# Choosing anew which groups VectorE makes, where they lie and which leave a step to GpSimd, with new pacing and scheduler constants, in a fused attention and FFN block

## The chip, the cores and the metric

One core of a Trainium2 chip runs the whole program. The metric is the device time of one execution in microseconds. Before the change the kernel took 773.14 us (median of three runs). PE is the matrix engine, ACT is ScalarE, DVE is VectorE, POOL is GpSimd. All runs told of here are of the state "fast".

## The reference, cut to what matters

```python
xn  = layernorm(x)                                   # 2048 x 512
qkv = xn @ wqkv                                      # 32 heads of 16
p   = softmax(q @ k.T / 4)                           # 32 heads x 2048 x 2048
A   = (p @ v) @ wo
h   = relu(xn @ W_gate) * (xn @ W_up)                # 2048 x 1792
out = x + A + h @ W_down
```

The exponential over 32 x 2048 x 2048 scores is the large job. ACT does most of it; the kernel gives a part to DVE.

## The kernel before: the parts that the change and the argument touch

A *group* is four heads x 512 queries x 128 keys: four tiles of 128 x 512. A *block* is one set of four heads and 512 queries, with 16 groups; there are 32 blocks and 512 groups. `D_POS` lists for each block the positions whose exponential DVE makes; all other groups go to ACT, as *units* of alternately three and two tiles. PV is the product of probabilities and V that consumes either kind; PE issues it in steps of four matmuls side by side. Units are counted from 0 in ACT's order.

```python
SLIP = 100.0                 # a tolerance in the scheduler, for GpSimd pieces beside DVE work
FILL = 0.72                  # below this share of PE work in a window, blank matmuls are put in
NRING = 6                    # places for finished exponentials: 6 of three tiles, 6 of two
P_PRIO = -2.4                # rank of GpSimd's pieces in the scheduler
POOL_AT = ((), (2,), (), (6,), ...)    # positions whose shifted pattern GpSimd makes
D_POS   = ((), (2, 3, 8, 11), (2, 8, 11, 15), ...)
PV_LAST = 10                 # over the last 10 units PV is preferred
O_BEG, F_PRE, F_BEG = 10, (1, 1, 1), 20     # pacing of output projection and FFN
```

DVE makes an exponential from bit patterns, in four evictions from PSUM and four passes over 128 x 2048:

```python
def dve_exp(g, u):
    for j, t in enumerate(t4):
        # PE: scores into one bank of ps_b            (L1202)
        # DVE: tensor_scalar, scores -> uint16 pattern (L1218), 4 per group
    # DVE: two pattern operations (L1229, L1231) and one product (L1233)
    if g in on_pool:
        # GpSimd: five tensor_tensor adds of about 205 int32 columns (L1237)
    else:
        # DVE: tensor_scalar add of SHIFT              (L1244)
    ...
```

ACT's exponentials write into the ring, and PV frees a place in it:

```python
tr = Tile("r%d" % u, P_ring[k0])                       # needs a free place
exp_ops[u] = G.op("ACT", 75 + 427 * n, ex, reads=[ts], writes=[tr], ...)      # L1279
G.op("PE", 225, pv, ..., prio=u + PV_LAG - (200 if u > NU - PV_LAST else 0))  # L1178
```

A list scheduler in the program turns all operations into one fixed order for each engine when the program is built; at run time each engine goes through its own order and waits on semaphores. So a constant such as `SLIP` does nothing on the chip but change that order.

The softmax here doesn't subtract the row's maximum and nothing guards it: scores larger than these inputs give would overflow.

## Time and profile before

| | before |
|---|---|
| median | 773.14 us (772.91 to 774.35) |
| profiled run | 771.55 us, span 769.8 us |
| ACT, exponentials alone | 737.6 us busy, 6.6 us idle ahead of them |
| DVE busy | 725.0 us |
| last exponential ends | 759.46 us |

The busy lines, the costliest groups, the stretches and ACT's waits are shown in the prediction. The end of the timeline gives the *tail*: after the last exponential come the last PV, two copies (L1105), sums, reciprocals, the spreading of them, the last projection, four adds, and the store. The lines are from the timelines of ACT and DVE in the kernel before; columns are start, length, instruction, and in brackets the idle time just before it and what ended it:

```profile
754.34 5.12 ACT L1279 ACTIVATE ring<-ps_sc 128x1536 bf16<-128x1536 f32 x5 [0.25 <-PE ps_sc L1202]
...
757.29 1.28 DVE L1244 TENSOR_SCALAR dring<-dring 128x2048 uint16<-128x2048 uint16 x2
...
761.11 0.75 DVE L1105 COPY Wv<-ps_b 128x256 f32<-128x256 f32 x2 [2.54 <-PE ps_b L1178]
```

### The profile page before, as it was taken

What the parts mean: (1) busy time and instruction counts of PE and PEld (TensorE: products, weight loads), DVE (VectorE), ACT (ScalarE), POOL (GpSimd) and SP (SyncE); (2) the same over time, 40 slices, a digit from 0 to 9 for tenths busy, and PEclk for the clock granted to TensorE, in tenths of its full rate; (3) what the DMA queues carried; (4) which work ended last, traced back from release to release, by engine and by line L of the source; (5) the groups of instructions that cost most, each with busy time, mean ns of one, the idle gap of its engine ahead of it and who ended that gap; (6) DMA issues with size and microseconds to landing.
All of it is one profiled execution on the core that took longest, in us unless ns stands there. A gap on an engine that the chain in (4) does not pass through costs nothing.

```text
span 769.8 us, 21666 instructions
## 1 busy us (share of the span) xinstructions
PE 748.2 (97%) x9482; PEld 228.2 (30%) x9482; DVE 725.0 (94%) x1132; ACT 746.0 (97%) x662; POOL 200.3 (26%) x253
## 2 busy tenths in 40 slices
PE   8999999999999999999999999999999999999997
PEld 3322322222222222222232222222222233222333
DVE  8699999999999899999988999998999979999696
ACT  6999999999999999999999999999999999999994
POOL 3112232422122232412323113232222223232120
PEclk9999999999999999999999999999999999999999
DMA  6312121202111122222220122232121113221100
GB/s 212 118 43 57 55 59 50 78 23 77 38 45 38 52 76 59 71 69 69 67 56 30 57 64 57 59 76 59 51 68 47 60 50 88 54 74 47 37 15 28
DMA packets 95757, 46.83 MB, mean 61 GB/s; under 512 B 69936, under 2 KB 91824, under 8 KB 95664
## 3 DMA queue, kind: packets, MB, share of 16 engines
q1 hardware_dynamic: 95664, 45.46, 21.5%
q8 instruction: 74, 1.21, 0.6%
q14 instruction: 19, 0.16, 0.1%
HBM read 36.70 MB, written 8.50 MB: 59 GB/s over the span
## 4 chain that ended last, share of the span: by engine, by line
DVE 48%; PE 42%; ACT 8%; issue 1%; DMA 0%; POOL 0%; DVEq 0%
DVE dring L1218 19%; PE ps_b L734 16%; PE ps_b L1178 12%; PE ps_sc L1202 11%; DVE dring L1233 8%; ACT ring L1279 7%; DVE dring L1229 5%; DVE dring L1231 4%; DVE dring L1244 3%; DVE up_sb L942 3%; PE ps_b L1202 2%; DVE hT L946 2%; DVE Wv L1112 2%; DVE qT L786 1%; DVE v_aug L828 1%
## 5 line engine op out<-in xcount | busy, mean ns | idle before, releaser
L1279 ACT ACTIVATE ring<-ps_sc 128x1536 bf16<-128x1536 f32 (+1 forms) x647 | 737.6, 1271 | 6.6 <-PE ps_b L1178 3.7
L1218 DVE TENSOR_SCALAR dring<-ps_b 128x512 uint16<-128x512 f32 x432 | 288.0, 683 | 16.7 <-PE ps_b L1202 15.4
L1202 PE MATMUL ps_sc<-qm,kT 32*128 32x512 bf16 x1616 | 260.5, 384 | 4.6 <-ACT ring L1279 2.8
L1202 PE MATMUL ps_b<-qm,kT 32*128 32x512 bf16 x432 | 161.9, 384 | 2.8 <-DVE dring L1218 1.8
L1178 PE MATMUL ps_b<-ring,v_aug 128*17 128x512 bf16 x1616 | 145.4, 381 | 5.7 <-DVE Wv L1112 4.6
L1233 DVE TENSOR_TENSOR dring<-dring 128x2048 bf16<-128x2048 bf16 x108 | 130.9, 1213 | 0.0
L1202 PEld LDWEIGHTS ps_sc<-qm,kT 32*128 32x128 bf16 x1616 | 62.0, 91 | 226.8 <-ACT ring L1279 196.9
L1130 POOL TENSOR_TENSOR rrec<-rsum,minus 128x16 f32<-128x16 f32 x30 | 93.2, 3106 | 110.3 <-DMA rsum<-Wv 110.3
L1140 POOL TENSOR_TENSOR x_sb<-Wv,rb 128x128 bf16<-128x128 f32 x100 | 45.8, 458 | 247.7 <-DVE dring L1233 87.8
L1178 PE MATMUL ps_b<-dring,v_aug 128*17 128x512 bf16 x864 | 79.5, 381 | 0.2 <-DVE dring L1231 0.2
L1178 PE MATMUL ps_b<-dring,vd 128*17 128x512 bf16 x864 | 78.6, 382 | 0.3 <-DVE dring L1233 0.2
L1229 DVE TENSOR_SCALAR dring<-dring 128x2048 uint16<-128x2048 uint16 x108 | 73.6, 683 | 0.5
L1231 DVE TENSOR_SCALAR dring<-dring 128x2048 uint16<-128x2048 uint16 x108 | 73.7, 685 | 0.0
L1237 POOL TENSOR_TENSOR dring<-dring,shift 128x205 int32<-128x205 int32 (+1 forms) x80 | 42.1, 527 | 108.9 <-DVE dring L1218 37.2
L734 PE MATMUL ps_b<-xnT,wus 128*32 128x512 bf16 x896 | 69.4, 384 | 0.5 <-DVE dring L1218 0.3
L734 PE MATMUL ps_b<-xnT,wgs 128*32 128x512 bf16 x896 | 69.3, 384 | 0.4
L1244 DVE TENSOR_SCALAR dring<-dring 128x2048 uint16<-128x2048 uint16 x92 | 62.0, 682 | 0.0
L1178 PEld LDWEIGHTS ps_b<-ring,v_aug 128*17 128x17 bf16 x1616 | 37.2, 89 | 64.7 <-issue 35.8
L1202 PEld LDWEIGHTS ps_b<-qm,kT 32*128 32x128 bf16 x432 | 38.5, 91 | 45.9 <-DVE dring L1218 29.8
L734 PE MATMUL ps_b<-Wd,hT 128*32 128x512 bf16 x672 | 49.4, 382 | 0.2
L942 DVE COPY up_sb<-ps_b 128x512 f32<-128x512 f32 x56 | 38.2, 681 | 0.0
L1178 PEld LDWEIGHTS ps_b<-dring,vd 128*17 128x17 bf16 x864 | 20.4, 89 | 33.9 <-issue 12.3
(111 smaller groups left out, 402.0 us busy)
## 6 DMA issues: line engine op xcount, KB each, us to landing
rb<-rec_scr SPq DMA_DIRECT2D x30, 256.0 KB
wus<-in_B_W_up_dram SPq DMA_DIRECT2D x56, 128.0 KB, 2.4
wgs<-in_B_W_gate_dram SPq DMA_DIRECT2D x56, 128.0 KB, 2.3
qm<-q_scr SPq DMA_DIRECT2D x30, 128.0 KB
o_scr<-x_sb SPq DMA_DIRECT2D x25, 128.0 KB
q_scr<-qT SPq DMA_DIRECT2D x17, 128.0 KB
xr_sb<-in_A_x_dram SPq DMA_DIRECT2D x16, 128.0 KB, 2.6
out_dram<-xn_sb SPq DMA_DIRECT2D x16, 128.0 KB, 1.9
```

Of the source, the lines that this page charges most:

```text
L734: ins = e.matmul(bank_of(tile, sub)[32 * j:32 * j + 32, :], st[:, 32 * j:32 * j + 32], mv, start=(i == 0), stop=(i == n - 1), tile_positio ...
L942: G.op("DVE", 610, lambda e: e.tensor_copy(up_sb[:, tup.slot, :], bank_of(tu)), reads=[tu], writes=[tup], prio=slots[1] + EV)
L1130: G.op("POOL", 3000, lambda e: e.tensor_tensor(rrec[:, par, :], rsum[:, par, :], minus[:, 0:1].to_broadcast([128, 16]), ALU.pow), reads=[t ...
L1140: o = G.op("POOL", 200 + 1080 // N_MUL, lambda e, a=w * k, b=w * k + w: e.tensor_tensor(oT_of(tn)[:, a:b], o_sb[:, to.slot, a:b], rb[:, tr ...
L1178: ins = e.matmul(ps_b[32 * j:32 * j + VN, 0, :], v, src[j][1](k), start=(first and k == 0), stop=(last and k == ways - 1), tile_position=( ...
L1202: return e.matmul(bank, kT[32 * j:32 * j + 32, gg, 128 * kt:128 * kt + 128], qm[32 * j:32 * j + 32, t_q[(c4, gg)].slot, ee, :], start=True ...
L1218: o = G.op("DVE", 610, lambda e, j=j, ts=ts: e.tensor_scalar(dring[:, tp.slot, 512 * j:512 * j + 512].bitcast(U16), ps_b[:, ts.slot, :], 0 ...
L1229: G.op("DVE", 600, lambda e: e.tensor_scalar(b(tm, U16), b(tp, U16), 0xFF80, None, op0=ALU.bitwise_or), reads=[tp], writes=[tm], prio=u - ...
L1231: G.op("DVE", 600, lambda e: e.tensor_scalar(b(tn, U16), b(tp, U16), 0xFF80, 1, op0=ALU.bitwise_and, op1=ALU.bitwise_or), reads=[tp], writ ...
L1233: G.op("DVE", 1140, lambda e: e.tensor_tensor(b(tm), b(tp), b(tm, I16), ALU.mult), reads=[tm, tp], writes=[tm], prio=u - 3, name="d5", loc ...
L1244: G.op("DVE", 600, lambda e: e.tensor_scalar(b(ts_, U16), b(tp, U16), float(SHIFT), None, op0=ALU.add), reads=[tp], writes=[ts_], prio=u - ...
L1279: return e.activation(ring[:, a:a + n, :], ps_sc[:, 3 * k0:3 * k0 + n, :], ACTF.Exp, scale=0.25)
```

## The change

Its intent: one group more on DVE (109 rather than 108), three more shifted patterns on GpSimd (19 rather than 16), other positions for several groups, and new constants for pacing and for the scheduler, all chosen together.

```diff
-P_PRIO = -2.4
-POOL_AT = ((), (2,), (), (6,), (), (1,), (), (2,), (), (3,), ..., (1,), (), (3,), (), (4,), (), (2,), (), (3,), (), (1,), (), (1,), (), (1,))
+P_PRIO = -6.0
+POOL_AT = ((), (), (), (6,), (), (1,), (), (2,), (), (4,), ..., (1, 10), (), (3,), (), (4,), (), (2,), (14,), (3,), (), (1,), (1,), (1,), (), (1, 8))
-    (), (2, 3, 8, 11), (2, 8, 11, 15), (6, 9, 10),
+    (), (2, 3, 8, 11), (2, 9, 11, 15), (6, 9, 10),
 ... (blocks 10 and 21 likewise: one position moved)
-    (1, 8, 14), (3, 4, 11), (1, 6, 10, 13), (1, 7, 12),
-    (1, 8, 9), (1, 8, 11), (1, 2, 6, 12), (1, 2, 8, 9),
+    (1, 10, 14), (3, 4, 10, 11), (1, 6, 10, 13), (1, 7, 12),
+    (1, 8, 9), (1, 8, 11), (1, 2, 6, 12), (1, 4, 8, 9),
-PV_LAST = 10
+PV_LAST = 14
-O_BEG = 10
+O_BEG = 6
-F_PRE = (1, 1, 1)
-F_BEG = 20
+F_PRE = (2, 2, 2)
+F_BEG = 24
-    SLIP = 100.0
+    SLIP = 200.0
-    FILL = 0.72
+    FILL = 0.76
```

The group `(3, 4, 10, 11)` in block 25 is the added one.

## The prediction

> **What bounds the kernel now.** I read the page's busy shares first, then the slices, the costliest groups, the list of who waited for whom, the table by stretches, and the timeline of the last 15 us.
>
> ```profile
> PE 748.2 (97%) x9482; PEld 228.2 (30%) x9482; DVE 725.0 (94%) x1132; ACT 746.0 (97%) x662; POOL 200.3 (26%) x253
> ...
> PEclk9999999999999999999999999999999999999999
> ...
> L1279 ACT ACTIVATE ring<-ps_sc 128x1536 bf16<-128x1536 f32 (+1 forms) x647 | 737.6, 1271 | 6.6 <-PE ps_b L1178 3.7
> L1218 DVE TENSOR_SCALAR dring<-ps_b 128x512 uint16<-128x512 f32 x432 | 288.0, 683 | 16.7 <-PE ps_b L1202 15.4
> ```
>
> Three engines look full, so the shares alone do not decide. PE is busy by a modelled end: four matmuls side by side take some 0.2 us more per four (the timeline starts the next four 0.21 to 0.22 us later), and 9482/4 x 0.216 = 512 us is its issue time, two thirds of the span. It also ran 204 blank matmuls, which it would not if it were short of time. ScalarE is the one without room: its 647 exponentials fill 737.6 us of union time with 6.6 us idle ahead of all of them together. The stretches say the same, stage by stage:
>
> ```profile
> core 0: us, PE busy (x) PEld busy (x) DVE busy (x) ACT busy (x) POOL busy (x), PEclk, DMA share, GB/s
> ...
> 150.00:250.00 100.00, 98.70 (x1213) 28.56 (x1211) 99.94 (x151) 99.72 (x89) 24.43 (x30) 1.00 0.17 46
> ...
> 350.00:450.00 100.00, 98.11 (x1222) 29.04 (x1225) 94.05 (x142) 99.64 (x88) 27.61 (x31) 1.00 0.19 54
> 450.00:550.00 100.00, 97.69 (x1217) 29.03 (x1213) 97.74 (x149) 98.05 (x87) 27.55 (x35) 1.00 0.25 65
> ...
> 600.00:650.00 50.00, 49.75 (x684) 15.26 (x683) 43.74 (x65) 49.73 (x45) 11.37 (x14) 1.00 0.22 61
> ...
> 760.00:765.00 5.00, 5.00 (x100) 3.05 (x92) 2.75 (x8) 0.00 (x0) 0.00 (x0) 1.00 0.00 0
> ```
>
> ACT is at 99.6% or more nearly everywhere; DVE is full in 150 to 250 but has 5.95 us free in 350 to 450 and 6.26 us in 600 to 650. The chain that ended last runs 48% through DVE and only 8% through ACT; I do not take that for a DVE bound, since an engine fed at ACT's pace stands on the chain whenever it happens to be full, and ACT hardly idles. So the time is: about 22.4 us to the first exponential, 737 us of exponentials, ACT's gaps, and a tail of 769.8 - 759.5 = 10.3 us after the last one. Where does ACT idle?
>
> ```profile
> ACT ring L1279 <- PE ps_b L1178: 3.7, 3, 1.7
> ACT ring L1279 <- PE ps_sc L1202: 1.2, 4, 0.6
> ...
> DVE dring L1218 <- PE ps_b L1202: 15.4, 19, 1.8
> DVE xnT L989 <- PE ps_b L734: 6.5, 2, 4.7
> ```
>
> Of 3.7 us in three waits on L1178 (probability times V), two are 1.7 us each: the timeline has them at 514.64 and 730.39. There the exponential has its scores but no free place in the six-deep ring, because the probability-times-V matmul that empties it stands too late in PE's order.
>
> **What the Trainium skill says.** "ScalarE: Activation LUTs", section Rules for kernel authors, budgets about 0.3 us per ACTIVATE plus 0.83 ns per element. The trace: 1483 ns for 1536 columns and 1060 ns for 1024, so 423 ns per 512, 0.83 ns each: it agrees on the slope; the fixed part of the record is 214 ns, and most of it overlaps (below). "VectorE: DVE Perf Modes", section Side-by-side, gives about 1224 ns for the 2x mode and 693 ns for the 4x mode at 2048 bf16: the trace has 1213 ns for the product (L1233) and 682 to 685 ns for the three pattern operations, which agrees. "SBUF — State Buffer", section Who interferes with whom, calls the port pair of VectorE and GpSimd an exclusive lock: GpSimd's multiplies idled 87.8 us behind L1233 alone, in keeping with it, though queueing on data is mixed in. "TensorE: Matmul & The Clock Gate", section What's actually happening, says that activity releases the throttle; here the granted clock is 1.00 in nearly all stretches, so more blanks have nothing to win.
>
> **The change part by part.** I compared the instruction streams of the two built programs, which tells counts and order and no time.
>
> (1) One group more on VectorE. A group is 4 heads x 512 columns. Exponentials go from 1616 tiles in 647 instructions to 1612 in 645: one of 1536 columns and the single one of 512 fall away. Start to start, the 49 exponentials listed at 63.13 in the chain took 55.89 us; 24.5 pairs give 2.28 us per pair, of which 5 x 0.423 is slope, so about 0.083 us fixed each. Saved on ACT: 4 x 0.423 + 2 x 0.083 = **1.86 us**, and this is on the bound.
>
> (2) What VectorE pays. The new group adds 4 evictions (L1218), two pattern operations, one product; the shifted pattern (L1244) falls from 92 to 90 because GpSimd takes 19 groups rather than 16. Back-to-back in the chain an eviction costs about 0.60 us (4.29 for 7), a pattern operation 0.60 (1.20 for 2), a product 1.13. So 2.4 + 1.2 + 1.13 - 1.2 = **+3.5 us** on DVE, whose idle between 25 and 755 us is over 30 us. The group is added in block 25 of 32. Counting 318 ACT groups ahead of it at 4 x 0.456 us from 22.4 puts the block at about 602 to 626 us, inside the stretch where DVE has 6.26 us free; its local cost, 5.3 us with its own shifted pattern on DVE, just fits. I book 0 on the path. PE gets 12 matmuls more for the group (four pieces of V for each D-group against one, and scores are unchanged in sum) and 32 blanks more: about 11 x 0.216 = 2.4 us, in slack.
>
> (3) GpSimd: 3 x 5 pieces x 527 ns = 7.9 us on an engine at 26%, zero on the path, unless a piece's late end holds a PV.
>
> (4) Places of groups and the FFN pacing change nothing in counts. What they move is order. In the streams I looked for exponentials whose last needed PE signal is not their own score but a later L1178, and counted matmuls between. Before there are five, by unit: 40 (27 matmuls late), 207 (23), 208 (39), 434 (42), 621 (48); the trace charges 0.24 us to the first, 1.71 and 1.69 us to the last two, nothing visible to 207 and 208. After there are four: 434 (28), 552 (21), 621 (15), 624 (32). By the only calibration there is (27 costs 0.24, 42 to 48 cost 1.7) I give 28 and 32 some 0.3 and 0.7 us and the shorter ones about 0.1 each: 1.2 instead of 3.65, **saving about 2.4 us**. This is my least sure term, as 39 matmuls cost nothing at 207/208.
>
> (5) The tail. Before, the last exponential ends at 759.46, but the last PV starts only at 760.45: after the last scores PE has eleven PV steps to issue, eight of them from VectorE's groups, since the last two shifted patterns (L1244) end at 758.6. Earliest possible would be about 759.7. After, with one of those patterns on GpSimd and PV preferred over the last 14 units, five PV steps follow the last scores. I take **0.8 us** of the 0.75 to 1.0 us there. The other tail steps (sums, reciprocal, spread, four output adds, DMA) are the same.
>
> Sum: 1.86 + 2.4 + 0.8 = 5.1 us. Against it I book 1.0 us for new small gaps: everything from the fifth block on stands in another order, and the gaps before are those of an already tuned order. Net 4.1 us: 773.1 - 4.1 = **769.0 us**, a ratio of 1.005.
>
> **The rivals.** (a) *Only the arithmetic counts*: reordered stalls come back elsewhere, and only the two exponentials are won: about 771.3 us. For it: 6.6 us of gaps spread over 647 instructions is close to a floor, and a static order shifts gaps rather than removes them. Against: the two 1.7 us gaps are single events with a named cause whose distance visibly shrinks. (b) *VectorE becomes the bound*: it is at 99.94% in 150 to 250 and 14.94 of 15 us in 730 to 745; the first block's shifted pattern returns to DVE, and in the after stream evictions stand closer to the end of the last block. If DVE falls behind, PE blocks at the head of its queue on a score bank, the next score comes late, and ACT idles. Worth up to the 3.5 us added: 772.5 to 775 us. Against: the free 6 us where the group goes, and in the last block one pattern leaves DVE. (c) *GpSimd's pieces hold the ring*: five pieces of 0.53 us, each likely to wait for a VectorE instruction of 0.6 to 1.2 us, make a shifted pattern ready some 5 to 8 us after its evictions; if PV waits, units stall as in the 1.7 us cases. PE's waits on L1244 and on GpSimd pieces are now small, and D-groups are begun ten units ahead; I give it 1 to 2 us at most. (d) *The extra wins all land*: gaps fall to about 2 us and the tail by 1 us: 765.5 us.
>
> **Range and chances.** 769.0 us, with 8 chances in 10 for **765.5 to 772.8**: the lower end is rival d, the upper lies between rivals a and b. Runs before spread over 772.9 to 774.4, so noise is under 1 us. Two per cent is 15.5 us; all ACT gaps, the group and the tail slack together are some 6.6 + 1.9 + 1.0 = 9.5 us, so faster by 2% is nearly excluded: 0.01. Slower by 2% needs a scheduling accident of 15 us: 0.01. Within 2%: **0.98**.
>
> **What would show it.** ACT's exponentials: 645, busy 735.7 us or within 0.4 of it; if busy falls less, step 1 is wrong. ACT idle behind L1178 at 0.8 to 1.6 us in place of 3.7: step 4. If gaps sum to 6 us or more, rival a; if ACT waits on L1202 scores grow by over 2 us together with DVE at 99% in 600 to 650 or 730 to 755, rival b. DVE busy near 729 us, GpSimd near 208: steps 2 and 3. Last exponential to end 9.5 us rather than 10.3: step 5. The prediction would be wrong most likely by the stall term, either way, as its calibration rests on three events.

## The result, and the profile after

The changed kernel took 766.78 us (four runs, 766.70 to 768.12) beside 773.02 us for the kernel before. The ratio is 0.9924, with a 95% interval of 0.9903 to 0.9945. Ratios here are the mean time of one kernel's fast runs over that of the other's of the same rounds, so they are not quite the ratio of the medians.

The page of the changed kernel: the busy line and the two groups that answer to those shown of before.

```profile
PE 747.8 (98%) x9526; PEld 228.0 (30%) x9526; DVE 729.1 (95%) x1137; ACT 744.4 (97%) x660; POOL 210.0 (27%) x268
...
L1279 ACT ACTIVATE ring<-ps_sc 128x1536 bf16<-128x1536 f32 (+1 forms) x645 | 736.1, 1266 | 4.3 <-PE ps_sc L1202 1.4
L1218 DVE TENSOR_SCALAR dring<-ps_b 128x512 uint16<-128x512 f32 x436 | 291.6, 682 | 16.0 <-PE ps_b L1202 15.1
```

The exponentials are 1.5 us shorter in sum, their idle time fell from 6.6 to 4.3 us. DVE carries 4.1 us more and waits as before. The list of who waited for whom, ACT alone (us in total, times, longest):

```profile
ACT ring L1279 <- PE ps_sc L1202: 1.4, 5, 0.6
ACT ring L1279 <- PE ps_b L1178: 1.3, 3, 0.5
```

The waits for a late PV went from 3.7 to 1.3 us, and the longest from 1.7 to 0.5. The waits for scores (both kinds of L1202) rose by 0.6 us, from 1.4 to 2.0. The stretches:

```profile
450.00:550.00 100.00, 98.53 (x1265) 29.59 (x1265) 97.61 (x148) 99.20 (x88) 26.27 (x32) 1.00 0.27 70
...
600.00:650.00 50.00, 49.41 (x657) 14.97 (x652) 45.44 (x68) 49.21 (x44) 11.94 (x14) 1.00 0.23 62
```

In 450 to 550 ACT gained 1.15 us of busy time (98.05 to 99.20), where one of the long waits had been. In 600 to 650, where the new group lies, DVE has 4.6 us free still. The end of the timeline:

```profile
747.83 7.91 ACT L1279 ACTIVATE ring<-ps_sc 128x1536 bf16<-128x1536 f32 x7
...
754.50 0.68 DVE L1244 TENSOR_SCALAR dring<-dring 128x2048 uint16<-128x2048 uint16 x1
...
756.24 0.76 DVE L1105 COPY Wv<-ps_b 128x256 f32<-128x256 f32 x2 [1.06 <-PE ps_b L1178]
```

Exponentials end at 755.74 (before: 759.46); the first copy follows 0.5 us later rather than 1.65. The rest of the tail is 8.7 us in both.

So the profiled runs, 4.9 us apart in span, split like this: exponential work -1.5, gaps -2.3, start +0.15 (the unit at 22.39 us starts at 22.54), tail -1.2. That is -4.85 us. The medians are 6.2 us apart; where the rest comes from is told at the last experiment.

### The profile page after: what moved, and what is told of

Same layout as the page of the kernel before. It is cut to its first block, busy times and chain, and to the rows that moved or that the text cites. A ratio compares the mean times of both kernels' runs of the same rounds, so it can differ in the third digit from the quotient of the medians.

```text
span 764.9 us, 21756 instructions
## 1 busy us (share of the span) xinstructions
PE 747.8 (98%) x9526; PEld 228.0 (30%) x9526; DVE 729.1 (95%) x1137; ACT 744.4 (97%) x660; POOL 210.0 (27%) x268
## 4 chain that ended last, share of the span: by engine, by line
DVE 51%; PE 45%; ACT 2%; issue 1%; DMA 0%; POOL 0%; DVEq 0%
DVE dring L1218 19%; PE ps_b L734 17%; PE ps_b L1178 12%; PE ps_sc L1202 12%; DVE dring L1233 8%; DVE dring L1229 5%; DVE dring L1231 4%; DVE dring L1244 4%; DVE up_sb L942 3%; PE ps_b L1202 2%; DVE hT L946 2%; ACT ring L1279 2%; DVE Wv L1112 1%; DVE kT L817 1%; DVE qT L786 1%
## 5 line engine op out<-in xcount | busy, mean ns | idle before, releaser
L1279 ACT ACTIVATE ring<-ps_sc 128x1536 bf16<-128x1536 f32 (+1 forms) x645 | 736.1, 1266 | 4.3 <-PE ps_sc L1202 1.4
L1218 DVE TENSOR_SCALAR dring<-ps_b 128x512 uint16<-128x512 f32 x436 | 291.6, 682 | 16.0 <-PE ps_b L1202 15.1
L1202 PE MATMUL ps_sc<-qm,kT 32*128 32x512 bf16 x1612 | 259.8, 384 | 2.4 <-ACT ring L1279 1.0
L1202 PE MATMUL ps_b<-qm,kT 32*128 32x512 bf16 x436 | 162.6, 384 | 1.3 <-DVE dring L1218 0.5
L1178 PE MATMUL ps_b<-ring,v_aug 128*17 128x512 bf16 x1612 | 144.8, 381 | 4.0 <-DVE Wv L1112 3.1
L1202 PEld LDWEIGHTS ps_sc<-qm,kT 32*128 32x128 bf16 x1612 | 61.8, 91 | 220.6 <-ACT ring L1279 193.9
L1237 POOL TENSOR_TENSOR dring<-dring,shift 128x205 int32<-128x205 int32 (+1 forms) x95 | 49.9, 525 | 117.8 <-DVE dring L1218 24.5
L1178 PE MATMUL ps_b<-dring,vd 128*17 128x512 bf16 x872 | 81.5, 382 | 0.3 <-DVE dring L1244 0.2
L1178 PE MATMUL ps_b<-dring,v_aug 128*17 128x512 bf16 x872 | 79.4, 381 | 0.0
L1178 PEld LDWEIGHTS ps_b<-ring,v_aug 128*17 128x17 bf16 x1612 | 36.6, 89 | 58.4 <-issue 34.9
L1202 PEld LDWEIGHTS ps_b<-qm,kT 32*128 32x128 bf16 x436 | 38.9, 90 | 49.1 <-DVE dring L1218 28.4
L1178 PEld LDWEIGHTS ps_b<-dring,vd 128*17 128x17 bf16 x872 | 20.6, 89 | 35.3 <-issue 13.3
```

The lines of the kernel that those rows point to most:

```text
L1178: ins = e.matmul(ps_b[32 * j:32 * j + VN, 0, :], v, src[j][1](k), start=(first and k == 0), stop=(last and k == ways - 1), tile_position=( ...
L1202: return e.matmul(bank, kT[32 * j:32 * j + 32, gg, 128 * kt:128 * kt + 128], qm[32 * j:32 * j + 32, t_q[(c4, gg)].slot, ee, :], start=True ...
L1218: o = G.op("DVE", 610, lambda e, j=j, ts=ts: e.tensor_scalar(dring[:, tp.slot, 512 * j:512 * j + 512].bitcast(U16), ps_b[:, ts.slot, :], 0 ...
L1237: o = G.op("POOL", 100 + int(P_NS * (z - a)), lambda e, a=a, z=z: e.tensor_tensor(b(ts_, mybir.dt.int32)[:, a:z], b(tp, mybir.dt.int32)[:, ...
L1279: return e.activation(ring[:, a:a + n, :], ps_sc[:, 3 * k0:3 * k0 + n, :], ACTF.Exp, scale=0.25)
```

## The experiments

The tool for all of them is a sum. In each profile the span is 15.3 us (head and ACT's other work), plus the busy time of the exponentials, plus the idle time just ahead of them, plus the tail from the last exponential's end. It holds within 0.2 us for all rows:

| kernel | median us | exp busy | idle before | of it behind L1178 | tail | span |
|---|---|---|---|---|---|---|
| before | 773.0 | 737.6 | 6.6 | 3.7 | 10.3 | 769.8 |
| changed | 766.8 | 736.1 | 4.3 | 1.3 | 9.2 | 764.9 |
| b_pvlast | 771.7 | 737.9 | 7.0 | 3.7 | 9.9 | 770.0 |
| b_slip | 768.6 | 738.4 | 3.6 | 0.2 | 9.3 | 766.5 |
| b_pvwin | 770.3 | 738.5 | 4.2 | 1.3 | 10.5 | 768.5 |
| b_group | 776.2 | 736.3 | 8.7 | 5.3 | 14.0 | 774.1 |
| a_nogroup | 770.3 | 738.3 | 4.8 | 0.3 | 10.3 | 768.6 |
| a_oldpool | 776.7 | 736.7 | 12.5 | 8.9 | 10.4 | 774.8 |
| a_ring5 | 782.9 | 736.7 | 17.6 | 11.7 | 10.2 | 779.9 |
| a_pace | 776.0 | 737.3 | 8.5 | 5.3 | 13.2 | 774.3 |
| b_fill | 773.0 | 738.0 | 7.9 | 3.7 | 10.3 | 771.5 |
| a_fill | 766.9 | 736.2 | 4.4 | 1.3 | 9.2 | 764.9 |
| a_ahead6 | 766.0 | 735.9 | 3.1 | 0.5 | 9.5 | 763.7 |

Names that begin with b are the kernel before with one edit, with a the changed kernel with one edit. All gave correct results.

The second tool is a count that needs no chip. In the built program I look, for each exponential, at the PE instruction whose signal it needs last. If that is not its own score but a PV further down PE's order, the PV is *late*, and the number of matmuls between the two says how late.

My theory: the gain is the exponential work removed, plus late PV removed, plus a shorter tail. The main rival: gaps only move about, and the extra group is the gain. A second rival: DVE's load is what counts. `P_PRIO`, the moved positions and `O_BEG` apart from the other pacing were not tested alone.

Medians mix runs that the clock slowed with runs that it did not (last experiments), and the kernel before is slowed more often. So for the small differences the spans of the profiled runs are the better measure: of these, only a_nogroup's and b_fill's were slowed. Both are given where they differ.

### One constant of the tail: b_pvlast

```diff
-PV_LAST = 10
+PV_LAST = 14
```

> The kernel before with PV preferred over the last 14 units rather than 10, nothing else; its streams differ only in the last block. After the last scores five PV steps follow instead of eleven. My theory (the tail of PV steps is on the path): last exponential to end 9.2 to 9.6 us instead of 10.3, so 0.7 to 1.1 us less than before, and the gaps of ScalarE unchanged (two waits of 1.7 us behind L1178). Rival (the tail is set by other steps, PV is hidden there): no change, within 0.3 us.

Median 771.71 us, ratio 0.9983 (0.9961 to 1.0006): no difference that can be told from noise, and the span is 770.0 against 769.8. The rival was right about the time, and not about the reason: the tail did shrink by 0.4 us, but ACT had waited just before it. The timeline of ACT, with its waits:

```profile
756.97 2.36 ACT L1279 ACTIVATE ring<-ps_sc 128x1536 bf16<-128x1536 f32 x2 [0.38 <-PE ps_sc L1202]
759.51 0.60 ACT L1279 ACTIVATE ring<-ps_sc 128x512 bf16<-128x512 f32 x1 [0.18 <-PE ps_sc L1202]
```

The steps of PV that were drawn forward, and with them the sums and the spread of the block before, stood ahead of the last scores. What left the tail came back as a wait for scores.

### One constant of the scheduler: b_slip

```diff
-    SLIP = 100.0
+    SLIP = 200.0
```

> The kernel before with only the tolerance SLIP raised from 100 to 200, which reorders the streams. The two exponentials with a PV 42 and 48 matmuls behind their scores are gone from the order, those at 40, 207, 208 stay, and two PV steps instead of eleven follow the last scores. My theory (late PV stalls and the tail): idle behind L1178 falls from 3.7 to about 0.3 us and the tail by 1 us: 3.5 to 4.5 us less than before. Rival a (gaps only move; only fewer exponentials count): no change, since it has the same 647 exponentials.

Median 768.60 us, ratio 0.9941 (0.9919 to 0.9962). This has the same 647 exponentials and the same groups, and gets 4.4 of the 6.2 us between the medians; between the profiled spans it is 3.3 of 4.9 us. Its waits:

```profile
ACT ring L1279 <- PE ps_sc L1202: 1.8, 7, 0.6
ACT ring L1279 <- PE ps_b L1178: 0.2, 1, 0.2
```

The late PV are gone as the count said, the gaps did not come back (3.6 us in all), and the tail is 1.0 us shorter. Against that the same 647 exponentials were busy for 0.8 us longer in sum. The rival that gaps only move has fallen, though a part did come back in this way.

### PV preferred where the two long waits are: b_pvwin

```diff
-prio=u + PV_LAG - (200 if u > NU - PV_LAST else 0)
+prio=u + PV_LAG - (200 if u > NU - PV_LAST or 418 <= u <= 436 or 605 <= u <= 623 else 0)
```

> The kernel before with PV preferred in two windows of units, 418 to 436 and 605 to 623, where the two 1.7 us waits are. The late PV at 434 and 621 vanish from the order, one at 640 (34 matmuls) is new; the tail has nine PV steps instead of eleven. My theory: 3.4 us of waits gone, up to 0.7 back at 640: 2.5 to 3.4 us less than before. Rival a: the gaps come back elsewhere, under 1 us less.

Median 770.34 us, ratio 0.9970 (0.9948 to 0.9992), 2.7 us less. Both long waits are gone; the new late PV, 34 matmuls late, cost what is shown in the third line, the only wait of ACT behind a PV after 65 us. The two waits of before, then the one of this run:

```profile
514.64 1.45 ACT L1279 ACTIVATE ring<-ps_sc 128x1536 bf16<-128x1536 f32 x1 [1.71 <-PE ps_b L1178]
730.39 1.02 ACT L1279 ACTIVATE ring<-ps_sc 128x1024 bf16<-128x1024 f32 x1 [1.69 <-PE ps_b L1178]
...
750.58 7.39 ACT L1279 ACTIVATE ring<-ps_sc 128x1536 bf16<-128x1536 f32 x7 [1.03 <-PE ps_b L1178]
```

This shows the cause directly: giving PE the PV in time at those two places removes those two gaps. What it earns is less than the gaps. The profiled spans are 1.3 us apart, not the 2.5 to 3.4 expected: gaps -2.4, tail +0.2, and the same 647 exponentials +0.9 us busy. Why they are busy for longer is not shown; records of exponentials overlap, so a start delayed by less than the overlap counts as busy time and not as a wait.

### The extra group alone: b_group

```diff
-    (1, 8, 14), (3, 4, 11), (1, 6, 10, 13), (1, 7, 12),
+    (1, 8, 14), (3, 4, 10, 11), (1, 6, 10, 13), (1, 7, 12),
```

> The kernel before with one group more on VectorE in block 25 and nothing else: 645 exponentials. Late PV at 434 (42 matmuls), 522 (50), 624 (39) instead of 434 and 621; eight PV steps in the tail instead of eleven. My theory: 1.86 us less for the exponentials, about 1 us more for the third late PV, up to 0.4 less in the tail: 0.8 to 1.8 us less than before. Rival a: 1.9 us less, as gaps do not count. Rival b (VectorE becomes the bound): no gain or up to 3.5 us more, with DVE at 99% between 600 and 650 us.

Median 776.15 us, ratio 1.0042 (1.0021 to 1.0062): slower by 3.1 us, and by 4.3 between the profiled spans, which only rival b had allowed for, and not for rival b's reason. DVE is at 45.12 of 50 us between 600 and 650 and at 19.83 of 25 between 730 and 755, not at 99%. The exponentials did get shorter by 1.3 us. The late PV came as counted (522: 50 matmuls, 624: 39):

```profile
514.63 100.45 ACT L1279 ACTIVATE ring<-ps_sc 128x1536 bf16<-128x1536 f32 x88 [1.72 <-PE ps_b L1178]
616.96 20.45 ACT L1279 ACTIVATE ring<-ps_sc 128x1536 bf16<-128x1536 f32 x18 [1.87 <-PE ps_b L1178]
...
735.38 16.17 ACT L1279 ACTIVATE ring<-ps_sc 128x1536 bf16<-128x1536 f32 x14 [1.47 <-PE ps_b L1178]
```

But most of the loss is a tail of 14.0 us. The new order made DVE do the last group of the last block so late that two of its evictions came with or after the last exponential. The DVE timeline:

```profile
759.70 0.69 DVE L1218 TENSOR_SCALAR dring<-ps_b 128x512 uint16<-128x512 f32 x1
761.03 0.69 DVE L1218 TENSOR_SCALAR dring<-ps_b 128x512 uint16<-128x512 f32 x1 [0.64 <-PE ps_b L1202]
...
764.10 0.69 DVE L1244 TENSOR_SCALAR dring<-dring 128x2048 uint16<-128x2048 uint16 x1
```

The last exponential ends at 760.07, and then PE and the copies wait for DVE's four passes. I had counted PV steps after the last scores (eight, fewer than before) and so expected a shorter tail; the count was of the wrong thing.

### The changed kernel without the extra group: a_nogroup

```diff
-    (1, 10, 14), (3, 4, 10, 11), (1, 6, 10, 13), (1, 7, 12),
+    (1, 10, 14), (3, 4, 11), (1, 6, 10, 13), (1, 7, 12),
```

> The changed kernel with the extra VectorE group of block 25 taken out again (108 groups, 647 exponentials), all else kept. In its order only one exponential has a late PV, at 434 (28 matmuls), where the changed kernel has four (434, 552, 621, 624, together 1.3 us of idle); five PV steps in the tail. My theory: 1.5 us more for the exponentials, 1.0 less idle: 0.2 to 0.9 us above the changed kernel. Rival (the extra group is the gain of the change): 1.5 to 2 us above it or more.

Median 770.32 us, 3.5 above the changed kernel where I expected 0.2 to 0.9. The number lies where the rival (the extra group is the gain) had put it; that the group by itself is the gain is excluded by b_slip, which gains without it, and b_group, which loses with it. The late PV did fall to 0.3 us, as counted. But the exponentials took 2.2 us more, the tail went back to 10.3 us, and the profiled run holds 1.1 us of an odd wait for scores, which is taken up under b_fill. Two of four terms moved as expected; the tail and that wait did not. In this order of groups, unlike in before's, the extra group is worth at least its ACT work: the fastest of its four runs, 768.86 us, is still 2.1 above the changed kernel.

### The GpSimd choice: a_oldpool

```diff
-POOL_AT = ((), (), (), (6,), ..., (1, 10), ..., (14,), (3,), (), (1,), (1,), (1,), (), (1, 8))
+POOL_AT = ((), (2,), (), (6,), ..., (1,), ..., (), (3,), (), (1,), (), (1,), (), (1,))
```

> The changed kernel with the GpSimd choice of before (one pattern in every second block, 16 in all; block 9 keeps position 4), all else kept. Its order has late PV at 40 (27 matmuls), 208 (71), 551 (60), 552 (91), 620 (54), 621 (66), 624 (24). Reading the waits so far as 0.054 us per matmul late less 0.8 us, and half of it where two follow each other, my theory (late PV) gives 5 to 8 us of idle behind L1178: 4 to 7 us above the changed kernel. Rival (VectorE's load decides): three patterns at 0.6 us, 1.8 us above it at most.

Median 776.67 us, 9.9 above the changed kernel, more than the upper end that I expected (7). ACT waits 8.9 us for late PV, in five waits (the sum was expected at 5 to 8):

```profile
257.71 118.62 ACT L1279 ACTIVATE ring<-ps_sc 128x1536 bf16<-128x1536 f32 x104 [2.87 <-PE ps_b L1178]
...
653.55 1.02 ACT L1279 ACTIVATE ring<-ps_sc 128x1024 bf16<-128x1024 f32 x1 [2.78 <-PE ps_b L1178]
655.49 55.05 ACT L1279 ACTIVATE ring<-ps_sc 128x1536 bf16<-128x1536 f32 x48 [0.92 <-PE ps_b L1178]
...
735.69 17.29 ACT L1279 ACTIVATE ring<-ps_sc 128x1536 bf16<-128x1536 f32 x15 [2.08 <-PE ps_b L1178]
```

They sit at the places counted: 208 (71 matmuls late), 551 and 552 (60, 91) and 620 (54); the fifth is 0.25 us at unit 40. Unit 621 (66), right after 620, waits no more. Three patterns back on DVE are 1.8 us of DVE work, with DVE still at 94% (731.6 us); the rest of the loss is order. The tail grew by 1.2 us as well.

### A shorter ring: a_ring5

```diff
-NRING = 6
+NRING = 5
```

> The changed kernel with five places in each ring of exponentials instead of six. Fourteen late PV in its order, of 16 to 104 matmuls (528: 104, 618: 62, 619: 74, 395: 43, 366: 39). My theory: by 0.054 us per matmul less 0.8 us, 9 to 14 us of idle behind L1178, so 8 to 13 us above the changed kernel. Rival (gaps have other causes than the ring): within 2 us of it.

Median 782.85 us, 16 above the changed kernel, where 8 to 13 were expected. ACT waits 11.7 us for late PV, within the 9 to 14 expected; the worst place (528, 104 matmuls late) cost 4.90 us. In addition it waits 4.1 us behind L1202, of which 3.28 are one wait at 174 us, which I did not foresee. There PE stood for 0.43 us behind an eviction of DVE (L1218) and for 0.21 behind DVE's copy of K (L817), while DVE was busy for all of 166.7 to 175.7 us: a wait of rival b's kind. A ring of seven would have been the cleaner test; I did not run one, as by my count it does not fit in memory.

### The old pacing: a_pace

```diff
-O_BEG = 6
-F_PRE = (2, 2, 2)
-F_BEG = 24
+O_BEG = 10
+F_PRE = (1, 1, 1)
+F_BEG = 20
```

> The changed kernel with the old FFN pacing (three constants). Nine late PV (76: 30, 77: 34, 536: 41, 552: 39, 623: 47, 624: 63, the rest 15) and twelve PV steps in the tail. My theory: 5 to 7 us of idle behind L1178 instead of 1.3, a tail 0.5 to 1 us longer: 4 to 6.5 us above the changed kernel. Rival (pacing only moves FFN work within slack): within 1 us of it.

Median 776.02 us, 9.2 above the changed kernel, where 4 to 6.5 were expected. Late PV cost 5.3 us, as expected; the tail is 13.2 us, 4 above, where I expected 0.5 to 1. Between the last exponential (761.15) and the first copy (765.66) there are 4.5 us. In them PE issues nine of the twelve steps of PV counted after the last scores, and also the end of a spread (L1070) and eight steps of an output projection (L1309), which I had not counted; at 0.216 us these eight are an estimated 1.7 us:

```profile
765.66 0.76 DVE L1105 COPY Wv<-ps_b 128x256 f32<-128x256 f32 x2 [3.10 <-PE ps_b L1178]
```

So the pacing of projection and FFN is no small part of the change: with the other constants as they are, the old pacing undoes more than all of the gain.

### What a late PV costs

Single late PV whose wait can be read in the traces, with the matmuls counted beforehand and the wait measured:

| run, unit | matmuls late | wait us | 0.054 x matmuls - 0.8 |
|---|---|---|---|
| before, 40 | 27 | 0.24 | 0.66 |
| changed, 434 | 28 | 0.34 | 0.71 |
| changed, 624 | 32 | 0.47 | 0.93 |
| b_pvwin, 640 | 34 | 1.03 | 1.04 |
| b_group, 624 | 39 | 1.47 | 1.31 |
| a_pace, 552 | 39 | 1.22 | 1.31 |
| a_ring5, 366 | 39 | 1.22 | 1.31 |
| a_pace, 536 | 41 | 0.83 | 1.41 |
| before, 434 | 42 | 1.71 | 1.47 |
| before, 621 | 48 | 1.69 | 1.79 |
| b_group, 522 | 50 | 1.87 | 1.90 |
| a_oldpool, 620 | 54 | 2.08 | 2.12 |
| a_oldpool, 208 | 71 | 2.87 | 3.03 |
| a_ring5, 528 | 104 | 4.90 | 4.82 |

The slope, 0.054 us, is 0.216 us for four matmuls side by side, the issue time read off the timeline in the prediction; the 0.8 was fitted by eye to the eight rows of before, the changed kernel, b_pvwin and b_group, which were known then. Of the six rows run afterwards, five came within 0.2 us of it (lags of 39, 39, 54, 71 and 104). It is an estimate with misses: it is 0.4 to 0.5 us too high for the lags of 27 to 32, 0.6 too high at unit 536 of a_pace, 39 matmuls at unit 208 of before cost nothing visible, 43 at unit 395 of a_ring5 show only 0.36 us, one unit earlier, and the changed kernel waits 0.53 us at unit 552 for 21. Why is open. Where two late PV follow each other, the second waits little or not at all (a_pace at 623 and 624, with 47 and 63: 1.62 us in one wait).

### Blanks, and the two groups of runs: after_again, b_fill, a_fill

The kernels' runs fall into groups, about 1.35 us apart: before at 771.7 and 773.0 (some at 774 to 776), the changed kernel at 766.7 and 768.1. In a_nogroup's profiled run, one of the upper group, the view by stretches shows why: the clock column is 0.83 and 0.82 in two stretches.

```profile
225.00:230.00 5.00, 5.00 (x64) 1.54 (x62) 4.98 (x8) 5.00 (x5) 0.00 (x0) 1.00 0.35 115
230.00:235.00 5.00, 3.99 (x38) 0.93 (x38) 4.53 (x7) 5.00 (x5) 2.13 (x5) 0.83 0.03 5
235.00:240.00 5.00, 5.00 (x65) 1.39 (x62) 4.09 (x7) 3.80 (x5) 2.58 (x1) 0.82 0.20 54
240.00:245.00 5.00, 5.00 (x60) 1.45 (x56) 3.76 (x6) 4.86 (x5) 1.84 (x4) 1.00 0.16 56
```

PE had waited 1.01 us there for a copy (L1112), then ran its matmuls at 0.6 us instead of 0.39 for some three microseconds, and the next score came 1.14 us late. The idle time alone does not bring this about: the changed kernel's profiled run has the same wait at the same place, with the clock at 1.00 throughout:

```profile
PE ps_b L1178 <- DVE Wv L1112: 1.0, 1, 1.0
```

To test whether more blanks prevent this, I changed the threshold alone, both ways, and ran the changed kernel again.

```diff
b_fill:                        a_fill:
-    FILL = 0.72               -    FILL = 0.76
+    FILL = 0.76               +    FILL = 0.72
```

> The changed kernel once more, unaltered, to size the gain: the kernels show runs in two groups some 1.35 us apart (before: 771.7 and 773.0). My theory: lower group 766.7, as in the profile 4.9 us under before's lower group; the rest of the 6.2 us between the medians is how often each kernel falls into the upper group. Rival: the gain is 6 us in both groups.

> The kernel before with only the filling threshold raised from 0.72 to 0.76: four blank steps more on PE, the order on every other engine the same. My theory (the upper group is one dip of the granted clock after PE idles near 1 us, as the profile of the changed kernel without its extra group showed at 231 us): lower group unchanged at 771.7 within 0.2, fewer than half of the runs in the upper group. Rival: blanks do nothing, as many upper runs as before has in the same rounds. Either way ScalarE's gaps and the tail stay as they are.

> The changed kernel with the filling threshold back at 0.72: twelve blank steps fewer on PE, the order on every other engine the same. My theory: lower group unchanged at 766.7 within 0.2, more runs in an upper group near 768.1. Rival (blanks are part of the gain): lower group rises by 0.5 us or more.

The changed kernel again: 766.96 us, four of five runs at 766.7 to 767.0, one at 768.4; ratio 0.9919 (0.9899 to 0.9940). a_fill: 766.88 us, five of six in the lower group. b_fill: 773.04 us, four of six between 772.9 and 773.8. So the threshold does nothing that these runs can show, neither to the gaps nor to the share of upper runs, and my guess about blanks was wrong. b_fill's profiled run (773.75 us) holds a dip too, at another place:

```profile
440.00:445.00 5.00, 4.69 (x41) 1.24 (x38) 5.00 (x10) 5.00 (x5) 1.96 (x1) 1.00 0.29 83
445.00:450.00 5.00, 5.00 (x53) 1.17 (x49) 4.37 (x7) 4.09 (x4) 0.94 (x1) 0.66 0.20 55
```

It follows a stretch with only 41 matmuls in 5 us, most of its steps scores for DVE with a single matmul each. The kernel before has the same stretch (42), and its profiled run did not dip there; the changed kernel has 59. 12 of 33 runs of before, and seven of nine of the changed kernel, lie in the lower group (the mark set at 772.3 and 767.3). The lower groups are 4.9 us apart, as the profiles are; the other 1.3 us between the medians is that before is slowed more often. That the dips cause all upper runs is likely and not shown, as only two upper runs were profiled. But each run's mean granted clock for the kernel before parts the groups: 29 runs list it, the 12 up to 772.6 us all at 0.999 or 1.000, the 17 above all at 0.998 or less, and those near 776 at 0.992 or 0.993. And of the 14 profiled runs here (after_again included), read in 5 us stretches up to 760 us, only these two show a clock below 1.00. A lower mean does not always cost time: b_slip's fastest run is at 0.998, and its profile has the low stretches after 760 us, where PE has little left to do.

### An attempt to beat both: a_ahead6

```diff
-D_AHEAD = 5
+D_AHEAD = 6
```

> The changed kernel with scores of VectorE's groups allowed six units ahead instead of five, an attempt to beat it: late PV at 207 (19 matmuls), 621 (15), 624 (32) only. My theory: idle behind L1178 from 1.3 to about 0.7 us, six PV steps in the tail instead of five: 0 to 1 us less than the changed kernel, 765.8 to 766.7. Rival (order shifts gaps, it does not remove them; tail or score waits grow): up to 2 us more.

Median 765.99 us, ratio to before 0.9909 (0.9889 to 0.9929). Idle time ahead of the exponentials is 3.1 us, late PV 0.5 us. Its lowest runs are at 765.6 against 766.7, and its span is 1.2 us under that of the changed kernel; the two intervals overlap, so it is better by the profile and unclear by the intervals. A second extra group was looked at by the count alone: each of some hundred built orders with a 110th group in one place or another had at least 7 us of late PV by the same rule, so none was run.

## Why the prediction was right, point by point

The time lay in the range (766.8 in 765.5 to 772.8) and the class was right; the point, 769.0, was 2.2 us too high. By its steps:

1. *Exponential work, -1.86 predicted.* Counts right (645). Busy time fell by 1.5 us between the profiles, by 2.2 between the changed kernel and the same without the group. Right as far as it can be read: kernels with the same 647 exponentials differ by up to 0.9 us (737.6 to 738.5).
2. *DVE, +3.5 us and none of it on the path.* DVE rose by 4.1 us. In the changed kernel it is hidden, as said. But the reason given, free time where the group lies, was not enough: the same group in the old order cost 3.1 us net (4.3 between the profiled spans), through the tail and late PV, with DVE just as free there. The step was right for this kernel and its argument incomplete.
3. *GpSimd, +7.9 us off the path.* It rose by 9.7 us to 210 (I had put 208), at 27%. Right.
4. *Late PV, -2.4 us.* 3.7 to 1.3 us: right in size, and b_slip and b_pvwin show the cause. It was called the least sure term, and by place there was luck in the sum: for units 434, 552, 621 and 624 it gave 0.3, 0.1, 0.1 and 0.7 us, and the trace has 0.34, 0.53, nothing and 0.47.
5. *Tail, -0.8 us.* It fell by 1.2 us. The size was about right, the mechanism not, so that was partly luck: fewer PV steps by `PV_LAST` alone gained nothing (b_pvlast), and tails of 10.3 and 14.0 us came with five and eight such steps (a_nogroup, b_group). What counts is how soon after the last exponential the first copy starts: 1.65 us before, 0.5 after.
6. *New small gaps, +1.0 us booked.* The idle time not behind L1178 was 2.9 us and is 3.0: +0.1. This term was mis-sized, by 0.9 us.
7. *Not in the sum:* how often a run is slowed by the clock, worth 1.3 us between the medians. The prediction read one profile with the clock at 1.00 and took that for all runs; it also called the noise under 1 us from three runs that spread over 1.4 us, while the profiled run it read (771.55) was already faster than all three.

Two readings were wrong without harm to the sum. The first exponential starts at 10.46 us and not at 22.4: six run before that. So the account of the time given there (22.4 + 737 + 6.6 + 10.3) exceeds the span by 7 us; what is left beside exponentials, gaps and tail is 15.3 us. And ACT is not at 99.6% nearly everywhere: the stretch of 450 to 550, shown there, is at 98.05.

The terms as measured give -4.9 us for the profiled pair, against -4.1; with point 7, -6.2. Of the rivals, a (only arithmetic) fell with b_slip, b (DVE becomes the bound) shows little in the changed kernel (waits for scores +0.6 us, where it asked for over 2) and c (GpSimd's pieces hold the ring) nothing (PE waits for no such piece there), and d (late PV and tail all won) was the nearest.

## What to carry to other kernels

Where one engine is busy to the last percent, write the span as its work, its gaps and the tail, and price a change in each of the three: here one scheduling constant won 4.4 us with no work removed, and one group of ACT's work removed lost 3.1 us (3.3 and 4.3 between profiled spans). In a statically ordered kernel, count in the built order how late each buffer is freed; in the experiments every wait of ACT behind a PV of over 0.5 us but one (0.82 us in a_ring5) lay at a place that this count had named, and the largest, 4.90 us, was forecast to within 0.1. Try the constants of such a schedule as a set: the new set won 6.2 us, and putting the old pacing or the old GpSimd choice back into it cost over 9.

## What the Trainium skill lacked or had wrong

- "TensorE: Matmul & The Clock Gate", section HAM oscillation, gives as abstract rule that PE should have no idle gaps over about 3.4 us; the page's section on a second failure mode also tells of a clock that oscillates under frequent shorter idle times. Here the granted clock fell (0.83 in one 5 us stretch and 0.82 in the next) after a single idle time of 1.01 us, and to 0.66 after a stretch with 41 matmuls in 5 us and no wait of PE over 0.21 us. Neither is enough: the same 1.01 us in the changed kernel, and the same stretch with 42 matmuls in the kernel before, passed in profiled runs at 1.00. What sets a dip off, in some runs of the same program only, is not shown. The groups of runs that dips probably explain lie 1.35 us of 770 apart.
- "ScalarE: Activation LUTs", section Rules for kernel authors, budgets about 0.3 us per ACTIVATE beside the 0.83 ns per element. The slope agrees (423 ns per 512 columns). The fixed part, for back-to-back exponentials out of PSUM, is 0.214 us in the record of one and only some 0.083 us from start to start; summing the records (647 x 1271 ns = 822 us) would exceed the span of 769.8 us, while the engine's busy time was 737.6 us.
- No page has a price for a place freed late in a ring between engines; here it was about 0.054 us per matmul of delay less 0.8 us, an estimate with the misses told above.
